# Tile 1's RMS norm from sums on all partitions, with tile 2's decay scans held behind it, and tile 0's decays made in halves, in a three-stage kernel on one core

## The chip, the cores and the metric

The kernel runs on one core of one Trainium2 chip. The metric is the device time of one execution in microseconds (us), the median of three runs. One further execution was recorded by the hardware profiler; all rows below come from that one. Its span, from the first to the last instruction of the core, is a little shorter than its device time.

The engines are called here as the profile calls them: PE is TensorE (matmuls; PEld is its weight loads), DVE is VectorE, ACT is ScalarE, POOL is GpSimd, SP is SyncE, which here only issues DMAs.

## What is computed

Three stages follow each other: a chunked linear attention with decays, a gated feed-forward layer behind an RMS norm, and a second feed-forward layer with a token shift. Cut to what matters:

```python
log_a = np.log(np.clip(a, 1e-06, 1.0))          # a: 4 batches, 8 heads, 768 positions
cum = np.cumsum(la, axis=-1)                    # per chunk
L = np.exp(cum[..., :, None] - cum[..., None, :]) * causal
M = np.einsum('bhin,bhjn->bhij', Cc, Bc) * L    # scores times decays
y = M @ xc + (Cc @ state) * np.exp(cum)[..., None]
state = decay_full * state + Bx                 # carried to the next chunk

rms = np.sqrt(np.mean(x * x, axis=-1, keepdims=True) + 1e-06)   # x: 3072 tokens x 256
xn = x / rms * rms_g
g = xn @ w_gate; silu = g * (1.0 / (1.0 + np.exp(-g)))          # 256 -> 1536
x2 = (silu * (xn @ w_val)) @ w_out                              # 1536 -> 256

xk = mu_k * x2 + (1.0 - mu_k) * x_prev; xr = mu_r * x2 + (1.0 - mu_r) * x_prev
k = np.maximum(xk @ w_k, 0.0)                                   # 256 -> 1024
out = (1.0 / (1.0 + np.exp(-(xr @ w_r)))) * (k * k @ w_v)
```

## The kernel before

The 768 positions are cut into six tiles of 128; a tile holds 128 positions of all four batches, so 512 columns (`T`). Tile t's first feed-forward layer (`ffn1`, 12 units of 128 hidden columns) runs on PE while the attention of tile t+1 is made beside it by small pieces hung between the units (`attend`, called by `hook("ab", u)` ahead of unit u). From tile 1 on the second feed-forward layer (`ffn2`) of the tile before follows.

Matmuls of the two layers are made of three products (`mm3`): weights and activations are split into a rounded part and a rest, as in `h` (an ACT cast makes the rounded part, a DVE subtraction the rest). One unit has six matmuls for `g`, six for `v`, and, two units later, six for `x` (`contract`), each of 512 columns. `g` goes through Silu on ACT (`sl`), DVE multiplies it by `v` (`hf`), and ACT and DVE split that into `h`. The results of `g` and `v` lie in four banks of the pool `pmm`, which are given out in turn: unit u's `g` takes the bank that unit u-2's `g` leaves when Silu has read it, and its `v` the bank that unit u-2's `hf` has read.

Weights arrive as 64-bit numbers and are turned into 32-bit pairs on ACT and DVE (`convert`): a clip on DVE (`wst`), two passes on ACT (`wst` and `wt`), a merge on DVE (`wt`), then casts on ACT and subtractions on DVE for the rounded part and the rest. `need(n)` in `hook` says how far this has to be at unit u (`NEED`).

Decays. For tiles 0 and 1 the decays are made from logs of `a`: `sums_e` makes the running sums and their rounded part `hi` and rest `v` on 128 partitions; then two tensors `right` and `left` are made from `v`, and `placed_e` multiplies each by 0/1 masks into `spread_r` (four blocks) and `spread_l` (two). `spread_e` adds the product of these two on PE to a causal mask (`spread_eye`, the bf16 matmuls `Eb<-before,eye`), for a pair of batches and both halves of the heads, and `exp_e` takes the exponential on ACT into `E`. For tiles from 2 on the decays come by a DMA and a scan on DVE (`e_scan`, 1024 columns, one a batch).

Norm. Tile 0's and tile 1's norm sums the squares of a token with matmuls that have the squares as weights and one column of ones as data (`rms_mm`), so the sums lie one a partition; a few tiny passes give 1/rms (`rms_a`, `rms_b`), and matmuls against a unit matrix spread it to all partitions (`rb`). For tiles from 2 on the ones are the weights and the squares the data, split in two parts, so one pass gives the sums on all partitions, and the passes are 128x512.

The order of the instructions on each engine is written by a planner in the kernel itself (`Order`, `arrange`): it runs through the program with prices and puts each engine's instructions in the order in which they then become ready. `chains` are extra edges for it, `urgent` marks instructions that go ahead. So a change of one step moves many instructions.

The tables that the change touches stand at the top: `VALUES` (the units of tile 0's feed-forward ahead of which a pair of batches of tile 1's attention is finished), `MEANS` and `SPREAD` (the units for tile 1's squares, sums and spreading), `NEED`, `START` (the steps ahead of the first unit, in order), `WARM` (matmuls on ones at the very start).

## Time and profile before

| | us |
|---|---|
| median of three runs | 508.61 |
| lowest and highest | 508.37, 509.46 |
| the profiled execution, device time | 508.6 |
| its span | 506.6 |
| PE busy in the span | 500.2 (99%) |
| DVE busy | 375.7 (74%) |
| ACT busy | 307.9 (61%) |
| POOL busy | 10.4 (2%) |

How to read it: the time outside the span (2.0 us) is the launch and the end. The profiled execution stands at the median. Matmuls overlap in their pipeline, so PE's busy time counts more than the steps from one start to the next; where a cost of PE is wanted, steps between starts are read, not durations. The same holds in a smaller measure on ACT and DVE: of two passes behind each other, the second starts about 0.1 us ahead of the first one's end.

### The profile page before, as it was taken

To read this page: it belongs to the slowest core of one execution; us is meant where nothing else is said; L and a number is where in the kernel's file an instruction comes from. 1 tells how busy PE (TensorE), PEld (TensorE's weight loads), DVE (VectorE), ACT (ScalarE), POOL (GpSimd) and SP (SyncE) were. 2 spreads that over 40 slices of the span, in tenths; PEclk is the share of its full clock that TensorE was granted. 3 is DMA by queue.
4 is the path that set the end of the run, shared out by engine and by line. 5 is a ranking of instruction groups with operands and counts; after the bars stand their busy time and mean duration, and the time that the engine had idled before them with its cause. 6 is when DMAs were issued, how large, how long until landed. Compare 5 with 4: busy or idle time off the path is not lost.

```text
span 506.6 us, 7497 instructions
## 1 busy us (share of the span) xinstructions
PE 500.2 (99%) x2869; PEld 406.8 (80%) x2869; DVE 375.7 (74%) x610; ACT 307.9 (61%) x509; POOL 10.4 (2%) x26
## 2 busy tenths in 40 slices
PE   8999999999999999999999999999999999999997
PEld 4687887788888888888888888888888888888885
DVE  6899998988698965479995659996628763335672
ACT  5999798566589744457763456764358643345552
POOL 1100000000010000010000010000000000000000
PEclk9999999999999999999999999999999999999999
DMA  8868755342321220152111141110000000000101
GB/s 257 230 204 276 261 175 193 105 137 93 123 85 43 78 82 13 57 174 77 42 58 68 46 162 44 65 48 36 0 1 1 18 25 1 1 1 0 42 0 42
DMA packets 23283, 42.60 MB, mean 84 GB/s; under 512 B 3136, under 2 KB 6720, under 8 KB 23248
## 3 DMA queue, kind: packets, MB, share of 16 engines
q1 hardware_dynamic: 20496, 33.41, 20.0%
q10 hardware_dynamic: 2752, 8.72, 5.1%
q8 instruction: 22, 0.36, 0.3%
q14 instruction: 13, 0.11, 0.1%
HBM read 38.52 MB, written 3.34 MB: 83 GB/s over the span
## 4 chain that ended last, share of the span: by engine, by line
PE 91%; DVE 5%; ACT 2%; issue 1%; DMA 1%; DVEq 0%; ACTq 0%
PE v L748 10%; PE v L750 10%; PE v L749 10%; PE g L748 6%; PE x L748 6%; PE x L749 6%; PE x L750 6%; PE g L749 6%; PE g L750 6%; PE kp L748 4%; PE kp L750 4%; PE kp L749 4%; PE y L527 2%; PE sc L442 1%; PE rps L750 1%; PE rps L749 1%
## 5 line engine op out<-in xcount | busy, mean ns | idle before, releaser
L792 DVE TENSOR_TENSOR hf<-sl,v 128x512 f32<-128x512 f32 x72 | 49.0, 683 | 50.0 <-PE v L750 49.5
L140 ACT CAST h<-hf 128x512 fp32r<-128x512 f32 x72 | 44.4, 617 | 60.8 <-DVE hf L792 60.7
L133 ACT ACTIVATE sl<-g 128x512 f32<-128x512 f32 x72 | 42.8, 595 | 44.9 <-PE g L750 44.6
L143 DVE TENSOR_TENSOR h<-hf,h 128x512 fp32r<-128x512 f32 x72 | 50.5, 701 | 24.1 <-ACT h L140 24.1
L748 PE MATMUL g<-xn,wgh 128*128 128x512 f32 (+1 forms) x148 | 58.0, 392 | 0.4 <-DVE E L514 0.4
L749 PE MATMUL g<-xn,wgl 128*128 128x512 f32 (+1 forms) x148 | 57.0, 385 | 0.4 <-DVE wgl L289 0.4
L748 PE MATMUL v<-xn,wvh 128*128 128x512 f32 (+1 forms) x148 | 57.0, 385 | 0.0
L750 PE MATMUL g<-xn,wgh 128*128 128x512 f32 (+1 forms) x148 | 56.8, 384 | 0.0
L749 PE MATMUL v<-xn,wvl 128*128 128x512 f32 (+1 forms) x148 | 56.8, 384 | 0.0
L750 PE MATMUL v<-xn,wvh 128*128 128x512 f32 (+1 forms) x148 | 56.8, 383 | 0.0
L749 PE MATMUL x<-h,wol 128*128 128x512 f32 x144 | 56.3, 391 | 0.0
L748 PE MATMUL x<-h,woh 128*128 128x512 f32 x144 | 55.8, 391 | 0.1
L750 PE MATMUL x<-h,woh 128*128 128x512 f32 x144 | 55.2, 389 | 0.0
L867 DVE TENSOR_TENSOR k<-rl 128x512 f32<-128x512 f32 x40 | 30.0, 749 | 15.0 <-ACT rl L863 15.0
L143 DVE TENSOR_TENSOR h<-k,h 128x512 fp32r<-128x512 f32 x48 | 32.8, 686 | 10.3 <-ACT h L140 9.9
L140 ACT CAST h<-k 128x512 fp32r<-128x512 f32 x48 | 29.7, 619 | 16.5 <-DVE k L867 16.3
L748 PE MATMUL kp<-xm,wkh 128*128 128x512 f32 x96 | 37.7, 393 | 0.0
L750 PE MATMUL kp<-xm,wkh 128*128 128x512 f32 x96 | 37.4, 390 | 0.0
L749 PE MATMUL kp<-xm,wkl 128*128 128x512 f32 x96 | 37.4, 389 | 0.0
L748 PE MATMUL v<-h,wvvh 128*128 128x512 f32 x96 | 37.3, 389 | 0.0
L749 PE MATMUL v<-h,wvvl 128*128 128x512 f32 x96 | 37.3, 389 | 0.0
L863 ACT ACTIVATE rl<-kp 128x512 f32<-128x512 f32 x48 | 28.5, 594 | 14.1 <-PE kp L750 13.4
(157 smaller groups left out, 983.0 us busy)
## 6 DMA issues: line engine op xcount, KB each, us to landing
E<-la_r ACTq DMA_DIRECT2D x16, 512.0 KB
x<-in_x_t SPq DMA_DIRECT2D x6, 512.0 KB
wst<-in_w_gate SPq DMA_DIRECT2D x6, 512.0 KB
wst<-in_w_val SPq DMA_DIRECT2D x6, 512.0 KB
wst<-in_w_out SPq DMA_DIRECT2D x6, 512.0 KB
Br<-in_B_s SPq DMA_DIRECT2D x12, 256.0 KB
Cr<-in_C_s SPq DMA_DIRECT2D x12, 256.0 KB
out<-r SPq DMA_DIRECT2D x11, 256.0 KB
```

Source lines behind the costliest of these rows:

```text
L133: one = nc.scalar.activation(out=out, in_=in_, func=func, **kw).ins.name
L140: last[1] = nc.scalar.copy(x[:, 0, :], src).ins
L143: last[0] = le.tensor_tensor(out=x[:, 1, :], in0=src, in1=f32(x[:, 0, :]), op=ALU.subtract).ins
L442: nc.tensor.matmul(bank[:, q * 256:(q + 1) * 256], bs[:, p, :], cs[:, p, :, :].rearrange("p a i -> p (a i)"), start=True, stop=True)
L527: nc.tensor.matmul(y[half][32 * j:32 * j + 32, at[half]:at[half] + P], x[:, b, h * D:(h + 1) * D], m[:, h, :], start=start and at[half] == ...
L748: nc.tensor.matmul(ps[:, s], w[0][:, k, ws], x[:, 0, s], start=first, stop=False, skip_group_check=s.stop - s.start < T)
L749: nc.tensor.matmul(ps[:, s], w[1][:, k, ws], x[:, 0, s], start=False, stop=False, skip_group_check=s.stop - s.start < T)
L750: nc.tensor.matmul(ps[:, s], w[0][:, k, ws], x[:, 1, s], start=False, stop=last, skip_group_check=s.stop - s.start < T)
L792: nc.vector.tensor_mul(hf, sl, v)
L863: marks.append(nc.scalar.activation(out=rl, in_=kp, func=AF.Relu).ins.name)
L867: nc.vector.tensor_mul(k2, rl, rl)
```

## The change

Tile 1's norm is made as for the later tiles: the squares of the two halves of the columns are added on DVE, split on ACT and DVE (`sqh`), and four matmuls of 256 columns with ones as weights give the sums on all partitions; then the 128x512 passes follow (Ln, Exp, Square on ACT; `ms`, `nw`, `rs` on DVE). The matmuls of one column and the four that spread 1/rms go. `MEANS` and `VALUES` put the attention's end and the norm earlier in tile 0's feed-forward. Tile 2's four scans wait, by an edge for the planner (`HELD`), for the last `xnf` of tile 1. `NEED[1]` and the loop in `need` make the conversions in tile 1 follow a table.

For tile 0 (and 1) the six blocks of `spread_r` and `spread_l` are made straight from `v`, one pass of 128x128 each, with a scale and a bias a partition, where `right` and `left` with two products stood; for tile 0 three on DVE and three on ACT. The decays go half by half of the heads: both batches of a pair for one half, then for the other. The first four unit-mask matmuls go ahead of the scores in `START`, and `WARM` falls from 9 to 5.

```diff
-VALUES = ((5, 6, 8, 10), (4, 6, 9, 11), (9, 10, 11, 12))
+VALUES = ((4, 5, 7, 8), (4, 6, 9, 11), (9, 10, 11, 12))
+HELD = (0, 1, 2, 3)
-NEED = ((4, 6, 8, 8, 10, 12, 12, 14, 16, 16, 18, 18, 18),
-        (99, 99, 99, 99, 99, 99, 99, 99, 99, 99, 99, 99, 99))
+NEED = ((4, 6, 8, 8, 10, 12, 12, 14, 14, 14, 18, 18, 18),
+        (20, 20, 20, 20, 20, 20, 22, 22, 24, 24, 26, 26, 99))
...
-START = 's0 k0 q0 q1 l0 p0 e0 ...
+START = 'q0 q1 s0 k0 l0 p0 e0 ...
-MEANS, SPREAD, LOAD_E = (6, 10), 11, (3, 6)
-WARM, COLD, HALVED, FILL = (9,), 11, 2, {('n', 0): 1, ('n', 2): 1}
+MEANS, SPREAD, LOAD_E = (8, 9), 11, (3, 6)
+WARM, COLD, HALVED, FILL = (5,), 11, 2, {('n', 0): 1, ('n', 2): 1}
...
     def placed_e(c):
...
+        def block(to, m, k, vector):
+            sc, cc = kcol(m + k), kcol(m + 6 + k)
+            if vector:
+                nc.vector.tensor_scalar(out=to, in0=v, scalar1=sc, scalar2=cc, op0=ALU.mult, op1=ALU.add)
+            else:
+                nc.scalar.activation(out=to, in_=v, func=AF.Identity, scale=sc, bias=cc)
+
+        for k in range(4):
+            block(spread_r[c][:, k], MP, k, c or k < RIGHT)
+        for k in range(2):
+            block(spread_l[c][:, k], MP, 4 + k, c)
...
     def e_scan(c, b):
         e = A[c]["E", b].rearrange("p h i -> p (h i)")
-        nc.vector.tensor_tensor_scan(out=e, data0=e, data1=cmask, initial=0.0, op0=ALU.mult, op1=ALU.max)
+        one = nc.vector.tensor_tensor_scan(out=e, data0=e, data1=cmask, initial=0.0, op0=ALU.mult, op1=ALU.max).ins.name
+        if c == 2 and b in HELD:
+            chains.append((spread[0], one))
...
-        if c > 1:
-            x, h = t2("sq"), pair("xn", "sq")
-            pool_e.tensor_tensor(out=x, in0=q[:, 0, :], in1=q[:, 1, :], op=ALU.add)
-            split(h, x, he, le)
-            q = [(ones, h[:, j, :]) for j in range(2)]
+        x, h = (q[:, 0, :], t2("sqh", F32R).rearrange("p (a i) -> p a i", a=2)) if c == 1 else (t2("sq"), pair("xn", "sq"))
+        (le if c == 1 else pool_e).tensor_tensor(out=x, in0=q[:, 0, :], in1=q[:, 1, :], op=ALU.add)
+        split(h, x, he, le)
+        q = [(ones, h[:, j, :]) for j in range(2)]
...
     def exps(c, b):
-        spread_e(c, (b, b + 1))
-        for k in (b, b + 1):
-            for half in range(2):
+        for half in range(2):
+            spread_e(c, (b, b + 1), half)
+            for k in (b, b + 1):
                 exp_e(c, k, half)
...
     def need(n):
-        if n > done[0]:
+        while done[0] < min(n, len(wjobs)):
             weights()
```

What this does to the orders, at three places. First DVE at the start, from the rest `v` of tile 0 to the first products `M` of scores and decays (`hv` holds `hi` and `v`, `a_104` the logs, `wvvh` and `wkh` lend their room to `spread_r` and `spread_l`). Before:

```order
L355 SCALAR_TENSOR_TENSOR hv<-hv,k_sb,a_104 128x128
L360 TENSOR_SCALAR hv<-hv,k_sb 128x128
L367 TENSOR_TENSOR wvvh<-hv,k_sb 128x512
L186 TENSOR_SCALAR a_104<-a_104 128x128
L353 SCALAR_TENSOR_TENSOR a_104<-ones,a_104 128x128
L354 CAST hv<-a_104 128x128
L355 SCALAR_TENSOR_TENSOR hv<-hv,k_sb,a_104 128x128
L360 TENSOR_SCALAR hv<-hv,k_sb 128x128 x2
L367 TENSOR_TENSOR wvvh<-hv,k_sb 128x512
L367 TENSOR_TENSOR wkh<-hv,k_sb 128x256
L514 TENSOR_TENSOR M<-sc,E 128x512 x8
```

And now:

```order
L354 SCALAR_TENSOR_TENSOR hv<-hv,k_sb,a_104 128x128
L362 TENSOR_SCALAR wvvh<-hv,k_sb 128x128 x3
L185 TENSOR_SCALAR a_104<-a_104 128x128
L352 SCALAR_TENSOR_TENSOR a_104<-ones,a_104 128x128
L353 CAST hv<-a_104 128x128
L354 SCALAR_TENSOR_TENSOR hv<-hv,k_sb,a_104 128x128
L362 TENSOR_SCALAR wvvh<-hv,k_sb 128x128 x4
L362 TENSOR_SCALAR wkh<-hv,k_sb 128x128 x2
L506 TENSOR_TENSOR M<-sc,E 128x512 x8
```

The products `M` stay behind all of tile 1's factors, which are six passes where four stood.

Second ACT in tile 0's feed-forward, around tile 1's norm (`sl` is Silu; the two table loads change from Silu's table to that of Ln and Exp and back). Before:

```order
L133 ACTIVATE sl<-g 128x512
L273 ACTIVATE wt_931<-wst_790 128x1024
L125 ACT_TABLE_LOAD
L140 CAST h<-hf 128x512
L288 CAST woh<-wt_931 128x512 x2
L581 COPY yT<-y 128x256 x2
L332 DMA E<-la_r 128x1024 x2
L662 ACTIVATE sq<-yT 128x512
L275 ACTIVATE wst_874<-wst_874 128x1024
L133 ACTIVATE tiny<-ss,k_sb 128x4
L133 ACTIVATE tiny<-tiny 128x4 x2
L125 ACT_TABLE_LOAD
```

And now, from the first load to the Silu behind the second:

```order
L124 ACT_TABLE_LOAD
L139 CAST h<-hf 128x512
L139 CAST sqh<-sq 128x256
L287 CAST wgh<-wt_976 128x2x256
L287 CAST wvh<-wt_976 128x2x256
L272 ACTIVATE wt_988<-wst_787 128x1024
L132 ACTIVATE rs<-ss,k_sb 128x512
L132 ACTIVATE rs<-rs 128x512
L132 ACTIVATE nw<-rs 128x512
L274 ACTIVATE wst_787<-wst_787 128x1024
L124 ACT_TABLE_LOAD
L132 ACTIVATE sl<-g 128x512
```

The three passes of the norm are 128x512 now, and more casts and conversion passes stand between the two loads. Before, the Silu ahead of the first load was that of unit 9 and the one behind the second that of unit 10; now these are units 8 and 9.

Third DVE behind tile 1's norm, from the split of `xn` to where tile 1's own units have begun (`E<-E,cmask` are tile 2's scans). Before, two of the four scans stood ahead of this place, among tile 0's units:

```order
L143 TENSOR_TENSOR xn<-xnf,xn 128x512 x2
L289 TENSOR_TENSOR wkl<-wt_1087,wkh 128x2x256
L143 TENSOR_TENSOR h<-hf,h 128x512
L289 TENSOR_TENSOR wkl<-wt_1087,wkh 128x2x256
L268 TENSOR_SCALAR wst_940<-wst_940 128x1024
L496 TENSOR_TENSOR Ch<-Ch,decay 128x512
L501 SCALAR_TENSOR_TENSOR E<-E,cmask 128x1024
L792 TENSOR_TENSOR hf<-sl,v 128x512
L279 SCALAR_TENSOR_TENSOR wt_1121<-wt_1121,wst_940 128x1024
L143 TENSOR_TENSOR h<-hf,h 128x512
```

Now all four stand behind it:

```order
L142 TENSOR_TENSOR h<-hf,h 128x512
L267 TENSOR_SCALAR wst_985<-wst_985 128x1024
L491 SCALAR_TENSOR_TENSOR E<-E,cmask 128x1024
L278 SCALAR_TENSOR_TENSOR wt_1088<-wt_1088,wst_985 128x1024
L769 TENSOR_TENSOR hf<-sl,v 128x512
L486 TENSOR_TENSOR Ch<-Ch,decay 128x512
L288 TENSOR_TENSOR wkl<-wt_1088,wkh 128x2x256
L491 SCALAR_TENSOR_TENSOR E<-E,cmask 128x1024
L288 TENSOR_TENSOR wkl<-wt_1088,wkh 128x2x256
L142 TENSOR_TENSOR h<-hf,h 128x512
L769 TENSOR_TENSOR hf<-sl,v 128x512
L491 SCALAR_TENSOR_TENSOR E<-E,cmask 128x1024
```

The first `h` of each is tile 0's last, and the `hf` behind it are tile 1's first; now the third scan follows the second of these, and the fourth comes later still.

On PE the block that finishes batches 2 and 3 of tile 1 (`y`) stands now behind unit 7 of tile 0, and the four `ss` matmuls stand behind unit 8's and inside unit 9's matmuls.

## Rows read from the trace of the kernel before

**Rows 1.** The page's busy time of each engine, share of the span, instructions
```profile
PE 500.2 (99%) x2869; PEld 406.8 (80%) x2869; DVE 375.7 (74%) x610; ACT 307.9 (61%) x509; POOL 10.4 (2%) x26
```

**Rows 2.** The waits of PE: engine line, waited for, us in total, times, longest
```profile
PE g L749 <- DVE wgl L289: 0.4, 1, 0.4
PE g L748 <- DVE E L514: 0.4, 1, 0.4
```

**Rows 3.** Timeline of DVE at the start: start us, us, engine line op, idle before
```profile
8.15 0.60 DVE L360 TENSOR_SCALAR hv<-hv,k_sb 128x128 fp32r<-128x128 f32 x2
8.67 0.68 DVE L367 TENSOR_TENSOR wvvh<-hv,k_sb 128x512 fp32r<-128x512 f32 x1
...
9.61 2.47 DVE L514 TENSOR_TENSOR M<-sc,E 128x512 f32<-128x512 f32 x4
13.16 1.29 DVE L514 TENSOR_TENSOR M<-sc,E 128x512 f32<-128x512 f32 x2 [1.08 <-PE sc L476]
```

**Rows 4.** Timeline of ACT at the start, tile 0's first exponentials
```profile
8.23 2.06 ACT L133 ACTIVATE E<-Eb 128x512 f32<-128x512 f32 x4 [1.22 <-PE Eb L393]
```

**Rows 5.** Timeline of ACT where tile 0's first units run
```profile
28.78 0.60 ACT L133 ACTIVATE sl<-g 128x512 f32<-128x512 f32 x1
29.27 0.61 ACT L288 CAST wgh<-wt 128x512 fp32r<-128x512 f32 x1
...
30.30 1.16 ACT L275 ACTIVATE wst<-wst 128x1024 int32<-128x1024 uint32 x1
31.34 0.60 ACT L133 ACTIVATE sl<-g 128x512 f32<-128x512 f32 x1
```

**Rows 6.** Timeline of PE, sums of tile 1's first half ahead of unit 7
```profile
56.83 1.05 PE L685 MATMUL ss<-ones,sq 128*128 128x1 f32 x8
57.74 0.48 PE L748 MATMUL g<-xn,wgh 128*128 128x512 f32 x1
```

**Rows 7.** Timeline of PE, the block that finishes batches 2 and 3
```profile
70.26 0.71 PE L569 MATMUL y<-Ch,Sf 64*128 64x128 f32 x8
...
72.14 0.50 PE L748 MATMUL g<-xn,wgh 128*128 128x512 f32 x1
```

**Rows 8.** Timeline of PE, sums of the second half and the spreading
```profile
75.23 0.39 PE L748 MATMUL x<-h,woh 128*128 128x512 f32 x1
75.46 0.95 PE L685 MATMUL ss<-ones,sq 128*128 128x1 f32 x8
76.27 0.49 PE L749 MATMUL x<-h,wol 128*128 128x512 f32 x1
...
78.21 1.12 PE L720 MATMUL rb<-tiny 128*128 128x128 f32 x8
79.09 0.47 PE L748 MATMUL g<-xn,wgh 128*128 128x512 f32 x1
```

**Rows 9.** Timeline of PE, two matmuls of 256 columns behind each other
```profile
25.70 0.28 PE L748 MATMUL v<-xn,wvh 128*128 128x256 f32 x1
25.82 0.28 PE L749 MATMUL v<-xn,wvl 128*128 128x256 f32 x1
```

**Rows 10.** Groups by line and shape: busy us, mean ns, idle before
```profile
L501 DVE TENSOR_TENSOR_SCAN E<-E,cmask 128x1024 f32<-128x1024 f32 x16 | 36.5, 2283 | 0.0
...
L711 DVE SCALAR_TENSOR_TENSOR nw<-nw,ms 128x512 f32<-128x512 f32 x4 | 2.8, 690 | 0.3 <-ACT nw L133 0.3
...
L133 ACT ACTIVATE rs<-ss,k_sb 128x512 f32<-128x512 f32 x4 | 2.7, 687 | 2.4 <-PE ss L680 2.4
...
L143 DVE TENSOR_TENSOR xn<-xnf,xn 128x256 fp32r<-128x256 f32 x4 | 1.6, 424 | 0.6 <-ACT xn L140 0.5
```

**Rows 11.** Timeline of ACT, the second table load of tile 1's norm
```profile
77.20 1.28 ACT L125 ACT_TABLE_LOAD   x1
78.50 1.13 ACT L273 ACTIVATE wt<-wst 128x1024 f32<-128x1024 f32 x1
79.53 0.59 ACT L133 ACTIVATE sl<-g 128x512 f32<-128x512 f32 x1
```

More of the change, by code (lines that the diff above doesn't have):

```diff
@@ L67, in shape_constants @@
     k[:, GL] = np.where(rest == 1, -1.0, 0.0)
-    k[:, SL], k[:, CL] = np.where(last == 1, -1.0, 0.0), last == 0
-    k[:, SR], k[:, CR] = last == 0, last == 1
+    for h in range(4):
+        k[:, MP + h], k[:, MP + 6 + h] = (last == 0) & (head % 4 == h), (last == 1) & (head % 4 == h)
     for j in range(2):
-        k[:, ML + j] = head // 4 == j
-    for h in range(4):
-        k[:, MR + h] = head % 4 == h
+        k[:, MP + 4 + j], k[:, MP + 10 + j] = np.where((last == 1) & (head // 4 == j), -1.0, 0.0), (last == 0) & (head // 4 == j)
     return k
@@ L383, in spread_eye, with spread_e @@
             A[c]["eye", b, half] = mm.ins.name
-    def spread_e(c, pair):
+    def spread_e(c, pair, half):
+        if ("Eb", pair[0], half) not in A[c]:
+            spread_eye(c, pair, half)
         for b in pair:
-            if ("Eb", b, 0) not in A[c]:
-                spread_eye(c, b)
-        for half in range(2):
-            for b in pair:
-                g = slice(32 * b, 32 * b + 32)
-                eyes = [A[c]["eye", k, half] for k in pair]
-                mm = nc.tensor.matmul(A[c]["Eb", b, half], spread_l[c][g, half], spread_r[c][g].rearrange("p h i -> p (h i)"),
-                                      start=False, stop=True)
-                chains.extend((one, mm.ins.name) for one in eyes)
-                if b % 2:
-                    costs[mm.ins.name] = 90.0
+            g = slice(32 * b, 32 * b + 32)
+            mm = nc.tensor.matmul(A[c]["Eb", b, half], spread_l[c][g, half], spread_r[c][g].rearrange("p h i -> p (h i)"),
+                                  start=False, stop=True)
+            chains.extend((A[c]["eye", k, half], mm.ins.name) for k in pair)
+            costs[mm.ins.name] = 90.0 if b % 2 else 228.0
     def exp_e(c, b, half):
-        if half == 0:
+        if ("E", b) not in A[c]:
             A[c]["E", b] = rp.tile([P, NH, P], F32, tag="E", bufs=4, name="E")
@@ L712, in rms_b @@
         nc.vector.scalar_tensor_tensor(out=r, in0=w, scalar=1.5, in1=r, op0=ALU.add, op1=ALU.mult)
[L713 to L723 removed]
+        if c == 0:
+            d["rs", s.start] = d["ss", s.start]
+            for k in range(2):
+                mm = nc.tensor.matmul(d["rs", s.start][:, k * P:k * P + P], r[:, k:k + 1].broadcast_to([P, P]), eye_f,
+                                      start=True, stop=True)
+            fill(d["rs", s.start][:, 2 * P:], FILL.get(("n", s.start // P), 0), [mm.ins.name])
     def xn_f(c, half, s):
@@ L925, in exps @@
     def exps(c, b):
-        spread_e(c, (b, b + 1))
-        for k in (b, b + 1):
-            for half in range(2):
+        for half in range(2):
+            spread_e(c, (b, b + 1), half)
+            for k in (b, b + 1):
                 exp_e(c, k, half)
@@ L982, in tile_kernel @@
     load_ch(1)
-    held = {}
+    held, spread = {}, []
     def soonest(f, *a):
@@ L1065, in attend @@
                         soonest(xn_f, c, half, full)
+                        spread[:] = urgent[-1:]
         def hook(kind, u):
```

70 lines of the change are left out of this document (18 added, 52 removed).

## The prediction

> **What bounds the kernel now.** I read the busy times first: PE is busy 99% of the span [rows 1]. So I asked next where PE still waits, and for whom. The table of its waits has two that lie inside the feed-forward layers, 0.4 us each, both on DVE [rows 2]: one for the weights of unit 2 of tile 0, one in tile 1 for products of tile 2's scores with its decays. From there to the end no matmul of PE waits. So the end is set by what PE has to do, plus what is lost in the first 100 us. An edit can win in three ways: fewer steps on PE, an earlier arrival at unit 2 of tile 0, or fewer waits before 101 us. DVE and ACT count only where PE waits for them.
>
> The sum is made against the profiled execution, 508.6 us (span 506.6 and 2.0 around it), which is the median of the runs.
>
> **Part 1, steps that leave and join PE.** Of the old norm of tile 1, the sums of the first half step from 56.83 to 57.74, 0.91 us [rows 6]; those of the second half from 75.46 to 76.27, 0.81, and the spreading from 78.21 to 79.09, 0.88 [rows 8]. All of it lies in a stretch where PE goes without a pause, so it counts fully: 2.60 us. In their place come four matmuls of 256 columns; the nearest rows step by 0.12 us [rows 9], so 0.48. Net: **-2.1 us**. If the new four stand badly among matmuls of another kind, each might cost 0.1 more; I take none, since their neighbours have the same kind of operands. All other matmuls are the same in number, but for the four warming ones at the start; those ran while nothing else was ready, and the four unit-mask matmuls that now follow them fill the same time.
>
> **Part 2, tile 0's start.** DVE makes tile 1's factors from 8.15 to 9.61 and begins the products M the moment it is free, with no idle time [rows 3]; the first exponential on ACT started at 8.23 and takes 0.6 of the four's 2.06 us [rows 4], so it was ready by 8.9, ahead of DVE. An earlier exponential, which the halves and the earlier unit masks give (I expect 0.5 to 1.1 us), meets the same queue: in the new order M still stands behind tile 1's factors. These are now six passes of 128x128; two of this shape start 0.52 us ahead of what follows [rows 3], 0.26 each, so 1.56 against 1.46 us before. Tile 0's three on DVE are shorter than what they replace by 0.2 or so, but tile 1's logs then wait for ACT, which makes its own three factors. So M begins at 9.6 again, give or take 0.1, and the fifth M, which waited 1.08 us for the scores [rows 3], waits for them again, since these wait for the first four.
>
> Later, at unit 2, ACT decides too. Silu of unit 0, at 28.78, stood ahead of the casts for unit 2's weights [rows 5]; now one more conversion pass (30.30 to 31.34, 1.04 us [rows 5]) stands ahead of the casts and both Silus behind them. Unit 2's first matmul takes the bank which Silu of unit 0 leaves, so that comes at the end of one pass and two casts more (1.04 + 1.03) and no longer at 29.4, around 31.4. That is near the moment at which PE, after its 0.4 us of waiting for DVE [rows 2], went on before. A gain of up to 0.8 us is open if ACT, which has its exponentials behind it sooner, is ahead by then; a loss of 0.6 if it isn't. I take **-0.1 us**.
>
> **Part 3, ACT around the norm.** The three tiny passes become 128x512 ones (0.69 us for the Ln of later tiles [rows 10], about 0.1 of it overlapped by the next pass, so 1.7 to 1.8 for three). That, two casts of 256 columns and the conversion passes stand between the two table loads, and Silu of unit 9 now stands behind the second one, where it was ahead of the first. PE needs that bank for unit 11. When does each come? PE: with the sums ahead of it gone, unit 7 begins at 56.83; its 18 matmuls step by 0.23 (the first two of [rows 8]), so 4.1 us; the block that finishes batches 2 and 3 follows, 1.88 us [rows 7], and ends at 62.9 with the change of kind. Then come units 8 and 9 with 18 matmuls each, the 12 of unit 10 and the four sums: 48 x 0.23 + 0.48 = 11.5, so PE wants unit 11's bank at 74.3 or 74.4. ACT, behind that block: two copies and two casts of 256 columns (0.42 by the DVE row of this width [rows 10], 0.32 as a step), two casts of h at 0.52, two for weights (1.03 together [rows 5]), two conversion passes `wt` and one `wst` at 1.04 [rows 5], Silu of unit 8 (0.49 [rows 5]), Square 0.52, the three passes 1.7, and two loads of 1.28 [rows 11]. Sum: 1.28 + 1.04 + 1.03 + 3.12 + 0.49 + 0.52 + 1.7 + 2.56 = 11.7. So Silu of unit 9 starts at 74.6 or later and frees the bank at 75.2: PE waits **+1.0 us**. From below the price is nothing (ACT works some of this off while PE is still in the block), from above 2.0, if ACT has to wait in that stretch for DVE's sums or merge.
>
> The Trainium skill speaks of the loads ("ScalarE: Activation LUTs", section "What ACT_TABLE_LOAD costs"): a load of about 1283 ns and a drain of about 1380 ns for every change of table. The load agrees with the 1.28 us of the row; the drain is not to be seen, since the next pass starts at 78.50, 0.02 us behind the load's end [rows 11]. By the row the term is 1.0, by the page's drain it would be 2 x 1.38 more, 3.8 us.
>
> **Part 4, DVE around the norm.** DVE gets three passes of 0.69 [rows 10] and four of 0.42 for sums and split, less three tiny ones: some 3.3 us more. But two scans of 2.28 [rows 10] leave the stretch ahead of the norm, and the first conversion of the second layer's weights (a clip of 0.6, a merge of 1.1, a subtraction of 0.6, as other passes of these widths step) comes later too, so tile 0's last h has 4.6 + 2.3 - 3.3 = 3.6 us less of DVE's work ahead of it. What that hides now is PE's own flow. Behind tile 0's last h, DVE has until tile 1's second hf: two scans (4.4 as steps), a merge (1.1) and seven passes of 0.6, 9.7 us; PE needs that bank for tile 2's scores after six groups of six matmuls and one of `x`, 9.6 us behind its first matmul of tile 1, which starts about 0.8 us behind that h. So it holds with some 0.5 us to spare, and the old wait there of 0.4 [rows 2] may halve: **-0.2 us**, between -0.4 and +1.0. The third sum matmul waits for a cast which follows the first load: +0.2 (0 to 0.5).
>
> What is queued with the moves: the copies of `y` and the DMAs of tile 2's decays that ACT issues behind them go earlier; nobody reads these before the held scans. SP's loads go in nearly the same order, with two columns more of constants, and no wait of PE hangs on them. POOL's queue is as it was but for one memset.
>
> **Sum.** 508.6 - 2.1 - 0.1 + 1.0 - 0.2 + 0.2 = 507.4; with the two blocks of [rows 8] goes also a slower restart of PE, whose pass behind a block takes 0.47 to 0.49 where one elsewhere takes 0.39, so 0.1 each and 0.2 in all: **507.2 us**.
>
> **Rivals.**
> - *ACT is not late.* The bank of unit 9 is free in time, the terms of 1.0 and 0.2 fall away: 506.0. For it: ACT is busy only 61% of the span [rows 1]. Against: the count above, which leaves it no gap.
> - *The first part works.* If the earlier exponentials let everything to unit 2 start 0.8 us sooner and not 0.1: 506.5. Against: DVE's unbroken row to 9.61 [rows 3].
> - *All is given back.* ACT's wait at its upper end, 2.0, and 0.5 for the sums: 508.5, no change.
> - *Slower: the held scans.* All four, 4 x 2.28 us, now fall into tile 1's first units. If DVE leaves tile 0's last h more than about 0.5 us later against PE than I have it, each scan ahead of an hf or h becomes PE's wait; one scan not hidden is 2.28 us: 509.5. Against: conversions have left that stretch.
> - *Slower by the table loads.* If each of the two loads held ACT for as long again as its row, now that passes of full width stand between them, Silu of unit 9 would come 2 x 1.28 us later, and PE's wait would grow by that: 509.8. Against: the row behind the load starts at once [rows 11]. By the drain of the Trainium skill's page "ScalarE: Activation LUTs" (section "What ACT_TABLE_LOAD costs") it would be 510.0.
>
> **How the numbers follow.** My forecast, 507.2 with its own range 506.6 to 507.8, has 0.42, of which 0.33 lies below 507.6; ACT in time 0.25; the start sooner 0.06; all given back 0.15; the scans 0.09; the loads 0.03. What a measurement can tell from no change is about 0.2%, 1.0 us. So faster 0.33 + 0.25 + 0.06 = 0.64, same 0.09 + 0.15 = 0.24, slower 0.12. The range reaches from 505.2 (ACT in time and the start's gain) to 508.8 (all given back) and leaves out the slower cases.
>
> **What would show it.** In the new profile: no `rb`, four `ss` of 256 columns that step by 0.12; M's first four again from 9.6 and the fifth from 13.2; a wait of PE on ACT's `sl` or an idle PE of about 1 us at unit 11 of tile 0, near 74; little idle time of PE between 90 and 101. I am wrong if PE never waits near 74 (then it is 506), if M starts well ahead of 9.6, or if PE waits on DVE's scans in tile 1.

## The result, and the profile after

| | before | after |
|---|---|---|
| median, us | 508.61 | 515.22 |
| lowest and highest, us | 508.37, 510.03 | 514.2, 521.96 |
| profiled execution, us | 508.6 | 514.2 |
| its span, us | 506.6 | 512.1 |

The change makes the kernel slower: the ratio is 1.0137 (95% interval 1.0112 to 1.0162). I had forecast 507.2 and at most 508.8. In some executions, of the kernel before too, the granted clock is low early on (in the traces that have it, at 0.50 for 3.4 to 17 us from 11.5 to 16.4 us on); the ratios leave such executions of the kernel before out but only some of the other kernels', so where ratio and medians part, the medians are followed.

The page's busy times, to be held against [rows 1], and the waits of PE, against [rows 2] (engine line, waited for, us in total, times, longest):

```profile
PE 500.4 (98%) x2845; PEld 405.7 (79%) x2845; DVE 377.9 (74%) x617; ACT 308.6 (60%) x511; POOL 9.4 (2%) x26
```

```profile
PE g L725 <- DVE hf L769: 2.9, 1, 2.9
PE g L725 <- ACT sl L132: 1.2, 2, 0.7
...
PE ss L645 <- ACT sq L643: 0.7, 2, 0.6
PE ss L668 <- DVE sqh L142: 0.7, 1, 0.7
```

No engine has much more work (DVE 2.2 us, ACT 0.7). PE waits, above all for four things that it didn't wait for before. To see what each costs, I set the start of the first matmul of each unit in one trace against the same matmul in the other. This lag, after minus before, is worked out from the two timelines of PE and sums to the 5.6 us between the profiled executions:

| up to | lag, us | grown by | I had |
|---|---|---|---|
| unit 3 of tile 0 | 0.91 | +0.9 | -0.1 |
| unit 1 of tile 1 (behind the norm) | 1.03 | +0.1 | -1.1 |
| unit 10 of tile 1 | 0.37 | -0.7 | -0.2 |
| unit 11 of tile 1 | 3.70 | +3.3 | 0 |
| unit 0 of tile 2 | 5.34 | +1.6 | 0 |
| the end | 5.57 | +0.2 | 0 |

**Tile 1, units 10 and 11** is where most went, 5.0 us of it, in a stretch that I had costed at nothing. PE's timeline there (start, us, engine line op, idle before and its releaser):

```profile
138.22 0.50 PE L725 MATMUL g<-xn,wgh 128*128 128x512 f32 x1 [2.94 <-DVE hf L769]
...
140.10 0.63 PE L726 MATMUL v<-xn,wvl 128*128 128x512 f32 x1
140.53 0.63 PE L727 MATMUL v<-xn,wvh 128*128 128x512 f32 x1
```

PE waits for `hf`. What did `hf` wait for? ACT's timeline, then DVE's:

```profile
131.59 1.20 ACT L274 ACTIVATE wst<-wst 128x1024 int32<-128x1024 uint32 x1 [3.41 <-DMA wst<-in_w_v]
132.67 0.59 ACT L132 ACTIVATE sl<-g 128x512 f32<-128x512 f32 x1
133.14 1.19 ACT L272 ACTIVATE wt<-wst 128x1024 f32<-128x1024 f32 x1
```

```profile
131.60 0.71 DVE L267 TENSOR_SCALAR wst<-wst 128x1024 f32<-128x1024 f32 x1 [2.59 <-DMA wst<-in_w_v]
134.36 1.23 DVE L278 SCALAR_TENSOR_TENSOR wt<-wt,wst 128x1024 int32<-128x1024 int32 x1 [2.06 <-ACT wt L272]
136.27 1.29 DVE L142 TENSOR_TENSOR xm<-xf,xm 128x512 fp32r<-128x512 f32 x2 [0.68 <-ACT xm L139]
137.48 0.68 DVE L769 TENSOR_TENSOR hf<-sl,v 128x512 f32<-128x512 f32 x1
```

Both engines stand still for a weight load. The Silu that `hf` reads is queued behind the conversion on ACT and ends at 133.3; `hf` itself stands on DVE behind the merge and the split of `xm`, which wait for ACT's passes in turn, and so comes at 137.48. The load landed at 131.6. It had been issued on SP's queue at 122.3 (here the row of 122.32 covers two issues, the second at 129.07, for other weights):

```profile
119.20 0.55 SPq L408 DMA_DIRECT2D Cr<-in_C_s  x1
119.79 0.54 SPq L408 DMA_DIRECT2D Br<-in_B_s  x1
121.91 0.37 SPq L245 DMA_DIRECT2D wst<-in_w_k  x1
122.32 7.12 SPq L245 DMA_DIRECT2D wst<-in_w_v  x2
```

Ahead of it stand two loads of tile 3's terms, 256 KB each, every one a broadcast of four copies. In the kernel before the same pair of weight loads was asked for at 102.1 and 102.5, ahead of the same term loads:

```profile
102.49 0.47 SPq L246 DMA_DIRECT2D wst<-in_w_v  x1
...
118.84 0.56 SPq L418 DMA_DIRECT2D Cr<-in_C_s  x1
```

The table by stretches (us, busy PE, PEld, DVE, ACT, POOL, then granted clock, DMA share, GB/s) shows the two speeds of that queue, and the clock behind the wait:

```profile
124.00:126.00 2.00, 2.00 (x11) 1.65 (x10) 2.00 (x4) 1.69 (x3) 0.00 (x0) 1.00 0.98 286
...
128.00:130.00 2.00, 2.00 (x10) 1.66 (x9) 1.01 (x2) 0.17 (x1) 0.00 (x0) 1.00 0.26 95
...
140.00:142.00 2.00, 2.00 (x6) 1.51 (x6) 2.00 (x6) 2.00 (x5) 0.00 (x0) 0.50 0.99 293
```

At 128 to 130, while ACT and DVE wait, DMA moves 95 GB/s on a quarter of its engines. And after PE's 2.9 us of idleness the granted clock falls to 0.50, the level of 1.2 GHz, from about 139.7 to 143.1: eight matmuls step by 0.43 instead of 0.23, which is 1.6 us, the whole next line of the table of lags.

**The start.** DVE answers to [rows 3]; then the third of ACT's squares for tile 0's norm, and PE's sums around it:

```profile
9.35 2.48 DVE L506 TENSOR_TENSOR M<-sc,E 128x512 f32<-128x512 f32 x4
13.23 1.89 DVE L506 TENSOR_TENSOR M<-sc,E 128x512 f32<-128x512 f32 x3 [1.41 <-PE sc L466]
```

```profile
15.91 0.38 ACT L643 ACTIVATE sq<-y 128x256 f32<-128x256 f32 x1 [1.16 <-PE y L519]
```

```profile
14.58 0.42 PE L519 MATMUL y<-M,x 128*32 128x128 f32 x6 [0.17 <-DVE M L506]
14.93 0.60 PE L645 MATMUL ss<-ones,sq 128*128 128x1 f32 x4
15.46 0.71 PE L519 MATMUL y<-M,x 128*32 128x128 f32 x12
```

The products stand where I had them. But the third square, at 15.00 before, is at 15.91: batch 2's products `y` are now cut in two by a row of sums (14.93), which takes PE 0.53 us; that this is the whole of the delay isn't shown. Unit 0's second half starts 0.8 us late, where its first half had been 0.5 early. At unit 2 a wait for ACT's Silu comes on top, so its first matmul is 1.45 us late:

```profile
32.19 0.50 PE L725 MATMUL g<-xn,wgh 128*128 128x512 f32 x1 [0.51 <-ACT sl L132]
```

Of this 0.91 is left at unit 3, since the old wait of 0.4 for `wgl` [rows 2] is gone. Two other traces with the old start, below, have a lag at unit 3 too, 0.43 (factors alone) and 0.87 (scans asked for earlier), because PE's first matmuls went more slowly there (16 scores in 1.83 and 2.27 us, before in 1.59). So one pair of traces doesn't fix the price of the start.

**The norm.** PE's four sums, then what came of unit 11 of tile 0, on PE and on ACT:

```profile
68.66 0.28 PE L668 MATMUL ss<-sqh,ones 128*128 128x256 f32 x1
69.63 0.38 PE L668 MATMUL ss<-sqh,ones 128*128 128x256 f32 x1 [0.69 <-DVE sqh L142]
69.85 0.40 PE L725 MATMUL g<-xn,wgh 128*128 128x512 f32 x1
...
70.77 0.39 PE L726 MATMUL g<-xn,wgl 128*128 128x512 f32 x1
71.30 0.38 PE L668 MATMUL ss<-sqh,ones 128*128 128x256 f32 x1
...
77.12 0.39 PE L727 MATMUL v<-xn,wvh 128*128 128x512 f32 x1
78.26 0.50 PE L725 MATMUL g<-xn,wgh 128*128 128x512 f32 x1 [0.74 <-ACT sl L132]
```

```profile
76.31 1.28 ACT L124 ACT_TABLE_LOAD   x1
77.61 0.60 ACT L132 ACTIVATE sl<-g 128x512 f32<-128x512 f32 x1
```

The second sum waits for DVE's rest of the split, the third for ACT's cast, which stands behind the table load. Unit 11 comes after a step of 1.14 where 0.23 is usual: 0.9.

### The profile page after: what moved, and what is told of

Same layout as the page of the kernel before. It is cut to its first block, busy times and chain, and to the rows that moved or that the text cites. A ratio compares the mean times of both kernels' runs of the same rounds, so it can differ in the third digit from the quotient of the medians.

```text
span 512.1 us, 7464 instructions
## 1 busy us (share of the span) xinstructions
PE 500.4 (98%) x2845; PEld 405.7 (79%) x2845; DVE 377.9 (74%) x617; ACT 308.6 (60%) x511; POOL 9.4 (2%) x26
## 4 chain that ended last, share of the span: by engine, by line
PE 88%; ACT 6%; DMA 2%; DVE 2%; issue 1%; DVEq 0%; SPq 0%; ACTq 0%
PE v L725 10%; PE v L727 10%; PE v L726 10%; PE g L725 6%; PE x L725 6%; PE x L726 6%; PE x L727 6%; PE g L726 6%; PE g L727 6%; PE kp L725 4%; PE kp L727 4%; PE kp L726 4%; DMA wst<-in_w_val 2%; PE y L519 1%; ACT E L132 1%
## 5 line engine op out<-in xcount | busy, mean ns | idle before, releaser
L142 DVE TENSOR_TENSOR h<-hf,h 128x512 fp32r<-128x512 f32 x72 | 49.5, 688 | 25.3 <-ACT h L139 25.3
L727 PE MATMUL v<-xn,wvh 128*128 128x512 f32 (+1 forms) x148 | 57.2, 387 | 0.0
L727 PE MATMUL g<-xn,wgh 128*128 128x512 f32 (+1 forms) x148 | 56.8, 384 | 0.0
L727 PE MATMUL x<-h,woh 128*128 128x512 f32 x144 | 55.7, 389 | 0.0
L142 DVE TENSOR_TENSOR h<-k,h 128x512 fp32r<-128x512 f32 x48 | 32.7, 684 | 8.4 <-ACT h L139 8.1
L727 PE MATMUL kp<-xm,wkh 128*128 128x512 f32 x96 | 37.4, 390 | 0.0
L491 DVE TENSOR_TENSOR_SCAN E<-E,cmask 128x1024 f32<-128x1024 f32 x16 | 36.5, 2283 | 0.0
```

The source lines that it names most:

```text
L142: last[0] = le.tensor_tensor(out=x[:, 1, :], in0=src, in1=f32(x[:, 0, :]), op=ALU.subtract).ins
L491: one = nc.vector.tensor_tensor_scan(out=e, data0=e, data1=cmask, initial=0.0, op0=ALU.mult, op1=ALU.max).ins.name
L727: nc.tensor.matmul(ps[:, s], w[0][:, k, ws], x[:, 1, s], start=False, stop=last, skip_group_check=s.stop - s.start < T)
```

## The experiments

Each was timed beside the kernel before on the same chip (its medians there: 508.6 to 509.0). "Ratio" is to that kernel, with its 95% interval.

### What makes the wait in tile 1

My first theory was that the late conversions (`NEED[1]`) alone make it.

**One pair of conversions in each unit,** as early as the planner's order in the kernel before has them:

```diff
-        (20, 20, 20, 20, 20, 20, 22, 22, 24, 24, 26, 26, 99))
+        (20, 22, 24, 26, 99, 99, 99, 99, 99, 99, 99, 99, 99))
```

> The changed kernel with one line undone: tile 1 converts one pair of weight tiles per unit again (units 0 to 3) instead of units 0, 6, 8, 10 and 12. Theory (late loads): the wait of 2.9 us at 135.3 on hf and the half-rate matmuls at 139.6 to 143.1 (about 1.6 us) go, so 514.4 - 4.5 to 5 = 509.5 to 510.0, and the trace shows no wait of DVE or ACT on the DMA of wst in that stretch. Rival (held scans): the four scans held behind tile 1's norm are what crowds DVE; conversions put back among them make it worse, so 514 to 517 with PE waiting on DVE near 90 to 105.

Median 513.09, ratio 1.009 (1.0073 to 1.0106). The wait at unit 11 is gone (the lag is 3.45 ahead of and behind it), but 2.0 of this lag arise between units 1 and 10. PE's longest waits are now `PE x L727 <- DVE h L142: 2.0, 2, 1.4`. DVE's timeline ahead of the longer one:

```profile
97.47 2.28 DVE L491 TENSOR_TENSOR_SCAN E<-E,cmask 128x1024 f32<-128x1024 f32 x1
...
100.85 0.68 DVE L142 TENSOR_TENSOR h<-hf,h 128x512 fp32r<-128x512 f32 x1
```

A held scan and two conversion passes stand ahead of an `h`. So four held scans do have the price of the rival in the prediction, once the conversions don't go out of their way. The last weight load is issued ahead of the term loads here (118.8 and 122.4).

**The scans not held,** `HELD = ()`:

```diff
-HELD = (0, 1, 2, 3)
+HELD = ()
```

> The changed kernel with the scans of tile 2's decays not held behind the norm, all else as changed. Theory (late loads): the conversions are as late as before, so the wait at 135 and the slow clock behind it stay: 514 to 515, within 0.7 of the changed kernel. Rival (held scans): most of the loss goes, 509 to 510.

Median 513.26, ratio 1.0096 (1.008 to 1.0113). Both forecasts missed: the wait in tile 1 goes, and the loss moves into tile 0's norm. The waits of PE (the profiled execution, 516.34, is the slowest of five, and in it the granted clock also stood at 0.50 from 76.4 to 79.8, behind these waits):

```profile
PE ss L668 <- ACT sqh L139: 2.2, 1, 2.2
PE g L725 <- ACT sl L132: 1.5, 2, 1.0
PE ss L668 <- DVE sqh L142: 1.1, 1, 1.1
```

**Late conversions in the kernel before,** nothing else:

```diff
-        (99, 99, 99, 99, 99, 99, 99, 99, 99, 99, 99, 99, 99))
+        (20, 20, 20, 20, 20, 20, 22, 22, 24, 24, 26, 26, 99))
...
-        if n > done[0]:
+        while done[0] < min(n, len(wjobs)):
```

> The kernel before with one line changed: tile 1's conversions at units 0, 6, 8, 10 and 12, as in the changed kernel. Theory (late loads): this alone brings the loss, since two loads of the second layer's weights then wait for a staging tile and land late: 508.6 + 3 to 5 = 511.6 to 513.6, with a PE wait of 2 to 3 us on hf between 125 and 145 and a granted clock under 1.0 behind it. Rival (held scans or the new norm): nothing, 508.6 within 0.5.

Median 510.22, ratio 1.0033 (1.002 to 1.0046): slower by 1.6, less than the theory had. The longest wait on the feed-forward's path is `PE g L748 <- DVE E L514`, 1.5 us, behind a merge whose load was late by 1.0. Lateness costs, but not 5 us; here that pair of weight loads was asked for at 112.7, ahead of the term loads. The pair before it stood behind two of them (96.4 and 97.0, then 97.7 and 98.2) and landed 10.5 us after its issue; ACT was idle for 4.2 us, but no matmul waited.

**Two conversions at every second unit,** in the changed kernel:

```diff
-        (20, 20, 20, 20, 20, 20, 22, 22, 24, 24, 26, 26, 99))
+        (20, 20, 22, 22, 24, 24, 26, 26, 99, 99, 99, 99, 99))
```

> The changed kernel with tile 1's conversions at units 0, 2, 4, 6 and 8: between the changed kernel (0, 6, 8, 10, 12; 3.3 us lost at 135 and 1.6 by the clock) and one per unit (3.1 us lost on h at 100 and 112). If both losses are prices of the same crowding, each is smaller here: no idle time of PE above 2 us, no half-rate matmuls after 120, 510 to 512. If only lateness counts (a load that lands late), it is 509.5; if only the scans count, 512 to 513 with the waits on h as before.

A miss: median 519.43, ratio 1.0233 (1.0174 to 1.0293). Earlier conversions, yet PE waits longer, 4.1 us. SP's queue, ACT, and a stretch:

```profile
118.98 0.56 SPq L408 DMA_DIRECT2D Br<-in_B_s  x1
120.05 0.55 SPq L408 DMA_DIRECT2D Cr<-in_C_s  x1
120.64 0.54 SPq L408 DMA_DIRECT2D Br<-in_B_s  x1
122.02 0.37 SPq L245 DMA_DIRECT2D wst<-in_w_v  x1
```

```profile
131.41 0.69 ACT L274 ACTIVATE wst<-wst 128x512 int32<-128x512 uint32 x1 [3.97 <-DMA wst<-in_w_v]
```

```profile
128.00:130.00 2.00, 2.00 (x10) 1.65 (x10) 0.00 (x0) 0.00 (x0) 0.00 (x0) 1.00 0.26 102
```

Three term loads stand ahead of one load of 512 KB, which lands 9.4 us after its issue. The share of 0.26 is also that of two term loads by themselves, in the kernel before:

```profile
122.00:124.00 2.00, 2.00 (x11) 1.65 (x10) 2.00 (x4) 1.99 (x4) 0.00 (x0) 1.00 0.26 102
```

This gave the second theory: it isn't how late the conversion is but what stands ahead of its load. A term load uses a quarter of the DMA engines, and the weights' part on those must wait for it.

The packets in the changed kernel's trace bear it out. Packets of 4 B can be read as the end of one DMA engine's part of a load: two term loads alone leave eight (the kernel before, 119 to 127), and the two term loads and two weight loads here leave 40 between 121 and 131.5, four for each of the first and sixteen for each of the others. Those of the term loads come by 124.2 and 127.3. Twelve of the first weight load's come by 126.1 and twelve of the second's by 128.5; the last four of each come only behind the terms, at 129.3 to 129.8 and at 130.6 to 131.1. The counts from 127.7 to 128.6, from 129.2 to 130 and from 130.5 to 131.3 (the last with another load's packets):

```profile
DMA packets 54, 0.09 MB, mean 96 GB/s; under 512 B 12, under 2 KB 12, under 8 KB 54
DMA packets 43, 0.08 MB, mean 100 GB/s; under 512 B 4, under 2 KB 4, under 8 KB 43
DMA packets 118, 0.23 MB, mean 292 GB/s; under 512 B 4, under 2 KB 4, under 8 KB 118
```

**The term loads behind the weights,** in the changed kernel, by an edge for the planner from the last weight load to tile 3's loads:

```diff
-            nc.sync.dma_start(out=r, in_=src[c, b].unsqueeze(0).broadcast_to([4, 32, T]))
+            names.append(nc.sync.dma_start(out=r, in_=src[c, b].unsqueeze(0).broadcast_to([4, 32, T])).ins.name)
...
+                elif c == 2:
+                    waiting.append((c + 1, two))
...
+            if u == NU:
+                while waiting:
+                    chains.extend((weight[0], one) for one in load_terms(*waiting.pop(0)))
```

> The changed kernel with the loads of tile 3's terms (Br and Cr, 256 KB each, on SP's queue) put behind the last load of the second layer's weights; the weights' own loads stay as late as they are (issued at 121.9 when their staging tile comes free). In the changed kernel two such term loads are issued at 119.2 and 119.8 and move at 102 GB/s on about a quarter of the DMA engines; the weight loads behind them land 9.2 us after their issue. Theory (the queue): without them the weights land some 4 us after issue, by 126.5, before ACT wants them at 128.2; the wait of 2.9 us and the slow clock of 1.6 us go: 514.4 - 4.5 = 509.9 (509.4 to 510.6). Rival (the late staging tile alone): the weights still land near 131, and the time stays at 513.5 to 515.

Median 510.91, ratio 1.0029 (1.0007 to 1.0051). The step from unit 10 to 11 is that of the kernel before (+0.00), and ACT's `wst` at 137.31 starts with no wait (the profiled execution, 520.63, was the slowest, with the granted clock at 0.50 from 11.8 to 28.8, so all of this stands some 10 us later in it). Behind unit 11 this kernel loses 1.5, of it 1.2 in a wait for an `h`. The edge also takes ACT's and DVE's work on those terms out of this stretch, so it doesn't single out the queue. **The same move with conversions at every second unit:**

> The same move in the kernel of e8_every_second (519.4), whose last weight load was issued at 122.0 behind three term loads and landed at 131.4, with 4.1 us of idle PE at 135 and 5 us of matmuls at the lower clock behind it. Theory (the queue): 6.9 us of loss go, so 512 to 513. Rival: the load's own place decides, 517 to 520.

Two executions timed, 517.58 (the profiled one, with the granted clock at 0.50 from 12.7 to 26.3) and 511.3; ratio 1.0109 (1.0056 to 1.0162). So its time says little; its trace says more. The wait of 4.1 is 0.5, units 10 to 11 grow by 0.73 and not by 6.92.

**The term loads in four pieces.** Their bytes, their place and the work on them stay; only the broadcast of four goes, for four DMAs of 32 partitions:

```diff
-            nc.sync.dma_start(out=r, in_=src[c, b].unsqueeze(0).broadcast_to([4, 32, T]))
+            for k in range(4):
+                nc.sync.dma_start(out=r[32 * k:32 * k + 32], in_=src[c, b])
```

> The changed kernel with one size changed: each load of tile 3's and later tiles' terms (Br, Cr, 256 KB), one DMA whose outermost dimension is a broadcast of 4 copies, becomes four DMAs of 32 partitions each. Order of the loads, staging tiles and conversions stay. In the changed kernel these loads move at about 102 GB/s with a DMA share of 0.26, a quarter of the engines, and the weight loads issued 2 to 3 us behind two of them land after 9.2 us. Theory (the quarter of the engines that still works off the term loads is what the weights wait for): spread over all engines a term load takes under 1 us, the weights land within 5 us of their issue, by 127, the wait of 2.9 us at 135 and the slow clock behind it go: 510.0 to 511.0, as with the terms put behind (510.9). Rival (it is the number of bytes ahead, or the late issue at 121.9): the same 0.5 MB stand ahead, landing and wait stay within 1 us, 513 to 515.

Median 509.94, ratio 1.0022 (0.9997 to 1.0048), where the changed kernel has 1.0137. Its lag is the changed kernel's up to unit 10 (0.38) and still 0.38 at unit 11, and 1.25 at the end. ACT and a stretch:

```profile
127.57 0.58 ACT L132 ACTIVATE sl<-g 128x512 f32<-128x512 f32 x1
128.24 1.18 ACT L274 ACTIVATE wst<-wst 128x1024 int32<-128x1024 uint32 x1
```

```profile
120.00:122.00 2.00, 2.00 (x10) 1.64 (x9) 2.00 (x4) 1.19 (x3) 0.00 (x0) 1.00 0.55 131
```

No wait, and no fall of the clock at 138 to 142. The Trainium skill ("DMA: Bandwidth & Descriptors", section "Rules for kernel authors") says that a DMA whose outermost dimension is smaller than 16, such as a leading broadcast of c copies, is confined to at most c engines; the shares agree, 0.26 for the broadcast of four and 0.55 or more in pieces. One thing else changed: of the two term loads one is now issued behind the weights (122.34), and the Silu stands ahead of the `wst`, since the planner had other prices. The one left ahead had its last packet at 122.0, where the undivided one had its at 124.2. So the cause is the term loads ahead of the weights; how much of the cure is the width and how much that one order, this run doesn't part.

### The start

**The old start in the changed kernel** (old factors, `START`, `WARM = 9` and the order by batches; some 80 lines go back):

```diff
-START = 'q0 q1 s0 k0 l0 p0 e0 ...
+START = 's0 k0 q0 q1 l0 p0 e0 ...
-WARM, COLD, HALVED, FILL = (5,), 11, 2, {('n', 0): 1, ('n', 2): 1}
+WARM, COLD, HALVED, FILL = (9,), 11, 2, {('n', 0): 1, ('n', 2): 1}
...
```

> The changed kernel with tile 0's decays made as in the kernel before (its own start undone), norm, held scans and late conversions as changed. The trace of the changed kernel puts +1.0 us on the new start (unit 2's second matmul at 32.5 instead of 31.5): 514.4 - 1.0 = 513.4, and unit 2 at 31.5. By my prediction's term for the start (-0.1) it would stay within 0.3 of the changed kernel, with the lost 1.0 us made up elsewhere.

Median 511.92, ratio 1.0073 (1.0047 to 1.01). It still has the wait of 2.9 in tile 1. By the ratios the start is worth 0.64%, 3.3 us, more than the lag of 0.9 behind it. Over the norm this kernel's lag shrinks by 0.6 (1.53 to 0.89), where the changed kernel's grows by 0.1. The rest can't be read from the one trace: it is that of the slowest execution, 514.22, with the granted clock at 0.50 from 16.4 to 19.8 and again behind the wait (139.3 to 142.7), while the two fastest, 510.99 and 511.38, have a mean granted clock of 1.00 and so neither stretch.

**The new start in the kernel before** is the reverse of that diff:

> The kernel before with the new start of tile 0 alone (decays by halves, factors straight from the logs); norm, scans and conversions as before. The changed kernel's matmuls stand 0.9 us later than before's from unit 3 of tile 0 on, so this theory gives 508.6 + 0.9 = 509.5 (509.2 to 510.0), with unit 2's second matmul at 32.5. My prediction's term (-0.1) gives 508.5; the rival in which the first part works 507.8.

Median 509.69, ratio 1.005 (1.0009 to 1.0092); lag at unit 3 is +1.24, and PE's sums of tile 0 wait 0.9 for squares. In the medians this is 0.7, as expected.

Which part of it? **The factors alone** (`placed_e` with one pass a block, the rest of before):

```diff
-        placed(right, spread_r[c], MR, 4)
+        for k in range(4):
+            block(spread_r[c][:, k], MP, k, c or k < RIGHT)
...
```

> The kernel before with the factors straight from the logs alone; the exponentials go by batches as before, and norm, scans and conversions are as before. The new start as a whole cost 0.9 us (e5_start_alone). If the cost lies in the order by halves (the sums of tile 0's norm placed between the products of batch 2), factors alone are at 508.6 within 0.4, with the exponentials 0.3 to 0.5 earlier; if it lies in ACT's three more factors ahead of tile 1's logs, it is 509.2 to 509.7.

Median 508.92, ratio 1.0000 (0.9986 to 1.0015): nothing. **The order by halves alone** (the loops, `START` and `WARM = 5`, old factors):

```diff
-        for k in (b, b + 1):
-            for half in range(2):
+        for half in range(2):
+            spread_e(c, (b, b + 1), half)
+            for k in (b, b + 1):
...
```

> The kernel before with the exponentials by halves alone (five warming matmuls, unit masks ahead, as in the new start), factors made as before. Factors alone cost nothing (e11_factors_alone, 508.9 beside 508.7), the whole new start 0.9. If the order by halves carries the cost, this one has it in full: 509.3 to 510.5; if only both together cost something, 508.6 to 509.0.

Median 510.38, ratio 1.0037 (1.0013 to 1.0062), in the range of the first. But it is lost elsewhere: +0.29 at unit 3, and then at units 5 and 6, where PE waits 0.5 for a cast of `woh` and 0.4 for `wol`. **Nine warming matmuls with the new start:**

```diff
-WARM, COLD, HALVED, FILL = (5,), 11, 2, {('n', 0): 1, ('n', 2): 1}
+WARM, COLD, HALVED, FILL = (9,), 11, 2, {('n', 0): 1, ('n', 2): 1}
```

> The kernel before with the new start alone (as in e5_start_alone) and nine warming matmuls instead of five; the planner then also puts the 16 products of batch 2 in a row, ahead of the sums of batch 1. Theory A (the products of batch 2 are cut by the sums, so ACT's third square is 0.9 late and the whole norm of tile 0 with it): the cost of the start falls from 0.9 to 0.3 or less, 508.6 to 509.0, with that square at 15.0 to 15.3 and no longer 15.9. Theory B (the cost lies elsewhere in the halves): 509.3 to 509.8 as with five. Of the two profiles in which the granted clock was at half level from 11 to 28, both had the new start with five warming matmuls: if the shorter warming is the cause, no execution here is above 513; if the pauses of PE at 7 to 12 are, some are near 516 again.

Median 509.17, ratio 1.0007 (0.9978 to 1.0037), between the ranges of the two theories. One of its twelve executions lies at 516.28, so by the test set above the shorter warming isn't the cause. Batch 2's products go in one piece again, the third square is at 14.26, and unit 0's second half is 0.58 early; by unit 6 all is given back (waits of 0.7 for Silu and 0.4 for `wol`). The number of warming matmuls thus moves the planner's order in the start.

### The norm, well placed

**Two scans behind the split only,** with the old start: the new norm of the change, the conversions one pair a unit, scans 2 and 3 held as in the change, scans 0 and 1 held only behind the split of the squares, and `NEED[0]` of before:

```diff
-HELD = (0, 1, 2, 3)
+HELD, EARLY = (2, 3), (0, 1)
...
+        elif c == 2 and b in EARLY:
+            chains.append((early[0], one))
```

> Old start, new norm; tile 2's first two scans held only behind the split of the sums (the other two behind the norm), tile 1's conversions one per unit as before. If the crowding of DVE in tile 1 is what the held scans and the late conversions trade against each other, moving one scan out of tile 1 frees both: no wait on a weight load, no wait on h, and the sum is 508.6 - 2.1 (PE's steps) + 0.9 (unit 11 of tile 0) + 1.0 (the sums' waits) - 0.7 (the two old waits of 82 and 100) = 507.7, between 506.7 and 508.6. Rival (early conversions collide with any held scans, as they did with four): 510 to 512, with waits of PE on h near 100.

Median 507.3, ratio 0.9976 (0.9966 to 0.9987): faster than before. What is left is a wait of 0.8 for a cast of `woh` and 0.6 for an `h` behind a scan.

**The same with the new start:**

> The kernel of e6_scan_behind_split with the new start of tile 0. If the start's price is its own, it stands 0.9 us above that kernel in the same comparison, about 508.6; by my prediction's term 0.1 below.

Median 510.31, ratio 1.0046 (1.0014 to 1.0077). Neither forecast held: the new start costs 3.0 here in the median and 0.7 in the kernel before. The lag is 0.94 at unit 3 and grows by 0.67 over the norm, where without the new start 1.60 is won; 0.8 of this difference are sums that wait for `sqh` again (0.4 each on ACT and DVE), the rest I did not follow.

**Scans asked for earlier,** on top of the first of these two:

```diff
-SCAN = ({3: (4,)}, {0: (0,), 1: (4, 1), 3: (2,), 5: (3,)})
+SCAN = ({3: (4,)}, {0: (0, 1), 1: (4,), 2: (2,), 4: (3,)})
```

> The kernel of e6_scan_behind_split with the scans written one unit earlier in tile 1 (0 and 1 at unit 0, 2 at unit 2, 3 at unit 4). There the fourth scan, 2.2 us on DVE at 105.3, stood between an hf and the h that PE waited 0.56 us for at 109.4. If DVE's order decides, that wait goes: 507.3 - 0.5 = 506.8 (506.4 to 507.3). Rival: an earlier scan only moves the wait to an h ahead of it, 507.3 or above.

Median 507.17 (506.11 to 507.8), ratio 0.9963 (0.995 to 0.9977): faster than both kernels, and the one I'd keep. The wait of 0.6 for an `h` is gone, though the median moved by 0.1 only. The sums stand among the matmuls around unit 9 without a wait; the third of them, which is 0.12 ahead of the next matmul:

```profile
70.67 0.28 PE L681 MATMUL ss<-sqh,ones 128*128 128x256 f32 x1
```

**This with the new start and nine warming matmuls:**

> The kernel of e10_scans_earlier with the new start and nine warming matmuls. The start alone with nine stood 0.6 us ahead at unit 0's second half and 0.5 us behind at unit 6 of tile 0, given back in waits on casts at units 4 to 6. If the giving back is a matter of ACT's load there (its casts and two extra conversions), it happens here too: 507.2 + 0.5 = 507.7 (507.2 to 508.3). If it was the order of that kernel alone, the gain carries through: 506.3 to 506.8.

Median 507.0 (506.17 to 509.73), ratio 0.9978 (0.9958 to 0.9999). Six executions lie at 506.2 to 507.3 and four at 509.2 to 509.7. No gain over the one before can be told.

## Why the prediction was wrong

**The step that failed** is in Part 4: "SP's loads go in nearly the same order, with two columns more of constants, and no wait of PE hangs on them." It cost nothing in the sum and 5.0 us in the profiled execution: 3.3 of waiting and 1.6 by the clock behind it. I had read `NEED[1]` as a relief of DVE (the conversions "come later too") and had counted DVE's passes, but not followed the loads. Those are issued when a staging tile comes free, and a later conversion frees it later: at 121.9 and 122.3, behind term loads of 119.2 and 119.8, where the kernel before had asked for the same pair at 102.1 and 102.5, and for its last weight load at 112.7, ahead of these term loads (118.8 and 119.4). The order of SP's instructions was there to be compared. The runs with the term loads out of the way (behind, or in pieces) take the wait away with the rest of the change in place, and the packets show the last quarter of each weight load behind the terms.

**The start** was sized at -0.1 and measured +0.9 in this trace. Its row held (M at 9.35, the fifth at 13.23), and so did Silu of unit 0 behind a further conversion pass (31.55); the step that failed was to follow DVE's products and ACT's Silu, and not the sums of tile 0's own norm, which share PE's queue with batch 2's products. Unit 2's first matmul came at 32.2 where I had 31.4: 0.8 of its lag stands at unit 0's second half already, and the wait for Silu, which I had named as a possible loss of 0.6, is the rest. The price isn't a constant: by the medians 0.7 in the kernel before, 3.0 with the well placed norm, 0.4 with nine warming matmuls, each time through another place of the order.

**The norm.** Right: `rb` is gone, four sums of 256 columns stand there, and unit 11 of tile 0 waits for Silu behind the second table load, +0.9 where I had +1.0. The size is partly luck: PE wanted the bank at 77.4 and not at 74.4, and the Silu started at 77.61 and not at 74.6, both 3 us later than counted. Mis-sized: the sums. From 68.66 to 69.85 is 1.19; from 70.77 to 71.53 is 0.76, less 0.23 for the step of `g`; the fourth takes 0.11. That is 1.83 where I had 0.48 and 0.2. I had asked only when the third one's cast comes, not when DVE has the rest of the first split: a merge of 1.22 stands ahead of it (68.02). So the stretch won nothing (+0.1), where 1.1 was forecast; in the version with well placed scans it wins 1.6 of the 2.1 that Part 1 had.

**Right in direction,** too small: the old wait of [rows 2] in tile 1 is gone, and the lag shrinks by 0.7 up to unit 10, where I had 0.2.

**The rivals.** The one of held scans was half right: its mechanism shows as soon as the conversions are early (a wait of 2.0 on `h` behind a scan of 2.28), and not in the change itself, whose late conversions make room. The table loads held ACT no longer than their rows, as [rows 11] had it: the Silu follows 0.02 us behind the load's end. ACT was late, and the start didn't gain. The one in which all is given back came true over the norm, but by the sums and not by a longer wait for ACT.

**Open:** how the gain of the pieces divides between width and order, and why the start costs 3 us in two of the surroundings. With the well placed norm the traces show where (0.9 at the start, 2.3 over the norm), but not why in full. In the changed kernel they show 0.9 and 0.8; the missing 1.6 is what the clock behind the wait costs, which two of the four executions with the old start didn't pay, but the one execution of the changed kernel with a mean granted clock of 1.00 took 514.43 all the same.

## What to carry to other kernels

When a table makes conversions later, follow the loads that feed them, not just the passes: their issue waits for a staging buffer, and then they join whatever queue stands there. On engines that work through their queues in order, as ACT and DVE do in these rows, one late load holds everything queued behind its first readers, here Silu and `hf` on two engines at once. And before an edit that gives work back is judged, place the work around it again: the same norm was worth +0.1 us in one order and -1.6 in another.

## What I had not expected of the hardware

- A load of 512 KB took 9.3 and 9.4 us from issue to landing behind two and three loads of 256 KB (and 10.5 in the kernel before with late conversions), and at most 5.8 when those stood behind it. These broadcasts of four move 102 GB/s at a DMA share of 0.26, where other stretches reach 286 at 0.98; three quarters of each weight load behind them were through 3.8 and 2.7 us ahead of the last quarter.
- After PE's 2.9 us of idleness at 135 to 138, the granted clock went to 0.50 only at 139.7, when PE had been back at work for 1.5 us, and stayed there for 3.4: the clock's price of 1.6 us came on top of the wait. It isn't paid each time: one of the six executions of this kernel has a mean granted clock of 1.00.
